# Moving the last eight heads of an output projection's weights behind the last V tile, the last ones head by head

## The chip, the cores and the metric

The kernel runs on one core of one Trainium2 chip. The metric is device time in microseconds (us), lower is better. A time is the median of several executions, every run fast, that is, not more than 1.5% above the fastest of its kernel. A profile is one execution. Its times count from the start of the span, and its span is some 2 us shorter than the measured time.

The engines are named as the profiler does: PE multiplies matrices (PEld is its loading of weights), DVE is the vector engine, ACT the scalar engine, POOL is hardly used here, and SP issues the loads, which the 16 DMA engines carry out. A load "lands" when the last of its engines has reported to the load's semaphore, a counter on which other engines wait. The "chain of waits" follows the work that ended last back from its end: at each step to what released it. PE's "granted clock" is given as a share of its full clock.

## The reference

One decode step of a transformer block for four sequences: attention over a cache of 8,192 positions, 32 heads of 128, in parallel with a gated feed-forward layer. All inputs are bf16.

```python
xn = layernorm(x)                                     # x: (4, 1, 512)
q = (xn @ wq).reshape(4, 1, 32, 128).transpose(0, 2, 1, 3)
p = softmax(einsum("bhqd,bhkd->bhqk", q, k_cache) * 128 ** -0.5)
o = einsum("bhqk,bhkd->bhqd", p, v_cache)             # caches: (4, 32, 8192, 128)
attn = o.transpose(0, 2, 1, 3).reshape(4, 1, 4096) @ wo      # wo: (4096, 512)
ffn = (silu(xn @ w_gate) * (xn @ w_up)) @ w_down
out = x + attn + ffn
```

The two caches are 537 MB, and wo is 4.2 MB. Everything has to be read once.

## The kernel before

The work is cut into 32 tiles of 4 heads of one sequence. K and V of a tile are 8.4 MB each and go through three large buffers in on-chip memory ("slots"). Every load is issued from SP's queue in program order, so the order of the calls is the order of the stream. The output of head `h` (`otn[:, h]`) is multiplied with the 128 rows of `wo` that belong to it, in four matmuls of 128 columns (`yo_mm`).

```python
def yo_mm(lhsT, rhs, start=False):
    for i in range(2):
        for a in range(2):
            c0 = a * DH + i * DQ
            mm(yo_ps[i][a * QB:a * QB + B, :], lhsT, rhs[:, c0:c0 + DQ], start=start)

def load_wo(t_):                       # heads 0..27 in 4 KB rows, heads 28..31 in 1 KB rows
    n = (NB4 - 1) * 4
    nc.sync.dma_start(out=t_[:, 0:n * D]..., in_=A_wo[0:n * P, :]...)
    nc.sync.dma_start(out=t_[:, n * D:H * D]..., in_=A_wo[n * P:H * P, :]...)
    wo_t.append(t_)
# ... tiles 0..30 in a loop; then the last one:
n = NT - 1
t_ = slot()
load_wo(t_)                            # wo
v_from(n, t_, H * D, 0, (T // 4, T // 4))   # first half of the last V, two loads
turn_k(n, (2,) * 8)
# ... scores of the last tile, PV of the tile before it
t_ = slot()
v_from(n, t_, 0, T // 2, (48, 32, 24, 16, 8))   # second half of the last V, five loads
max_1(n)
pv_still(n - 1, xps, T - 96, T)
max_2(n)
wo_some(H)                             # the 28 heads that are finished
pt_turn(n)
row_sums(n)
fin_1(JL)
pv_still(n, xps, 0, T - TL)
fin_2(JL, xps, B - 2)
pv_still(n, xps, T - TL, T)
fin_3(JL, xps)                         # normalise: otn of the last four heads
wo_ready = H
wo_some(H)                             # their product with wo
# ... copy yo_ps to res, store res in two halves (from SP and from ACT)
```

Of the kernel before, what the change touches and what calls it, by code (L numbers as in the profile page):

```python
# [15 lines left out]
def kernel(  # L16
# [13 lines left out]
    nc = tc.nc  # L30
    P = nc.NUM_PARTITIONS

    B, Sq, D = A_x.shape
    _, H, Sk, Dh = A_k_cache.shape
# [42 lines left out]
    def slot():  # L77
        return slots.tile([P, SLOT], dt.bfloat16, name="slot")
# [7 lines left out]
    def beside_wq(parts, w, dtype=dt.bfloat16):  # L86
# [13 lines left out]
                      in_=x_flat[B - 1:B, :].rearrange("b (k e) -> b k e", k=2))  # L100
# [13 lines left out]
    def v_from(n, t_, base, t0, parts):  # L114

        j, b = divmod(n, B)
        src = A_v_cache[b, j * HT:(j + 1) * HT, :, :].rearrange("h (p t) d -> (h p) (t d)", t=T)
        v_tiles[n, t0 * Dh] = (t_, base)
        for w in parts:
            nc.sync.dma_start(out=t_[:, base:base + w * Dh], in_=src[:, t0 * Dh:(t0 + w) * Dh])  # L120
            base, t0 = base + w * Dh, t0 + w
# [149 lines left out]
    NB4 = H // 4  # L271
    wo_t = []

    def load_wo(t_):
        n = (NB4 - 1) * 4
        nc.sync.dma_start(out=t_[:, 0:n * D].rearrange("p (k c e) -> p k (c e)", c=4, e=D),
                          in_=A_wo[0:n * P, :].rearrange("(k p c) e -> p k (c e)", p=P, c=4))
        nc.sync.dma_start(out=t_[:, n * D:H * D].rearrange("p (h e) -> p h e", e=D),
                          in_=A_wo[n * P:H * P, :].rearrange("(h p) e -> p h e", p=P))
        wo_t.append(t_)  # L280


    s_ps, pt, nmx, osb, rcp = {}, {}, {}, {}, {}
# [28 lines left out]
    def max_1(n):  # L312
        mx = small.tile([P, 1], dt.float32, name="mx")
        nc.vector.reduce_max(out=mx[:], in_=s_ps[n][:], axis=AX.X)  # L314
        nmx[n] = mx

    def max_2(n):

        mps = psM.tile([P, 512], dt.float32, name="mps")
        nc.tensor.matmul(mps[:, 0:P], lhsT=nmx.pop(n)[:, 0:1].to_broadcast([P, P]), rhs=ident_f[:, :],  # L320
                         is_transpose=True, start=True, stop=True, skip_group_check=True)
        nm = small.tile([P, HT], dt.float32, name="nm")
        nc.vector.tensor_reduce(out=nm[:], in_=by_row(mps[:, 0:P]), axis=AX.X, op=ALU.max, negate=True)  # L323
        nc.vector.tensor_tensor(out=nm[:], in0=nm[:], in1=rowb_q[:], op=ALU.mult)
        nb = small.tile([P, 1], dt.float32, name="nb")
        nc.vector.reduce_sum(out=nb[:], in_=nm[:], axis=AX.X)
        p_ = pp.tile([P, 512], dt.bfloat16, name="p_")
        rs = small.tile([P, 1], dt.float32, name="rs")
        nc.scalar.activation(out=p_[:], in_=s_ps.pop(n)[:], func=ACT.Exp, bias=nb[:, 0:1], scale=qscale,  # L329
                             accum_out=rs[:])  # L330
        pt[n] = p_
        rs_t[n] = (rs, mps)

    def pt_turn(n):
        p_ = pt[n]
        t_ = ptz[n % 2]
        for y in range(HT):
            nc.vector.transpose(out=t_[y * QB:(y + 1) * QB, :, y, :, :].rearrange("p s u x -> p s (u x)"),  # L338
                                in_=p_[y * QB:(y + 1) * QB, :].rearrange("p (s w) -> p s w", s=4))
        pt[n] = t_[:].rearrange("p s y u x -> p (s y u x)")  # L340
# [20 lines left out]
    def pv_still(n, xps, t0, t1, start=False):  # L361

        for t in range(t0, t1):
            k, u = divmod(t, NV)
            off = p_off(k) + u * QB
            mm(xps[:, :, n % B], v_cols(n, t * Dh, (t + 1) * Dh),
               pt[n][:, off:off + (HT - 1) * NV * QB + 1:NV * QB], start=(start and t == t0))
# [14 lines left out]
    def fin_3(j, xps):  # L382
        nc.vector.tensor_tensor(out=otn[:, j * HT:(j + 1) * HT, :], in0=xps[:], in1=rcp.pop(j)[:], op=ALU.mult)  # L383
# [12 lines left out]
    def wo_mm(i):  # L396
        yo_mm(otn[:, i, :], wo_t[0][:, i * D:(i + 1) * D])
# [7 lines left out]
    def wo_some(n):  # L405
        nonlocal wo_next
        while n > 0 and wo_next < wo_ready:
            wo_mm(wo_next)
            wo_next += 1
            n -= 1  # L410
# [47 lines left out]

    n = NT - 1
    t_ = slot()  # L460
    load_wo(t_)
    v_from(n, t_, H * D, 0, (T // 4, T // 4))
    turn_k(n, (2,) * 8)
    xps = x_tile()
# [3 lines left out]
            pv_still(n - 1, xps, (g - 7) // 2 * 32, (g - 5) // 2 * 32, start=(g == 7))  # L468
    t_ = slot()
    v_from(n, t_, 0, T // 2, (48, 32, 24, 16, 8))  # L470
    max_1(n)
    pv_still(n - 1, xps, T - 96, T)
    max_2(n)
    wo_some(H)
    pt_turn(n)
    row_sums(n)
    fin_1(JL)
# [1 line left out]
    fin_2(JL, xps, B - 2)  # L479
    pv_still(n, xps, T - TL, T)  # L480
    fin_3(JL, xps)
    wo_ready = H
    wo_some(H)
    assert wo_next == H
# [35 lines left out]
```

## Time and profile before

| | before |
|---|---|
| median of 3 runs (range) | 1285.74 us (1285.46 to 1285.93) |
| span of the profiled run | 1283.9 us |
| DMA | 551 MB at 430 GB/s |
| PE, DVE busy | 79%, 57% of the span |
| last V piece reaches PE | 1279.71 us |
| last matmul with wo ends | 1281.39 us |
| store issued by SP | 1281.70 us |

The DMA engines have no pause until the very end, so a change in the order of the loads can gain only in the last few microseconds, after the stream. The lines of the profile for this are shown and read in the prediction below.

### The profile page before, as it was taken

The page shows a single profiled execution, that of the slowest core. Times are in us where ns is not written, and L with a number is a line of the kernel's source. Part 1 is how long each engine was busy: PE and PEld are TensorE (multiplying, and loading weights), DVE is VectorE, ACT ScalarE, POOL GpSimd, SP SyncE. Part 2 cuts the span into 40 slices and gives each one's busy share as a digit, 9 for nine tenths or more (in the row PEclk, how much of TensorE's full clock was granted, in tenths as well). Part 3 has the DMA queues.
Part 4 walks back from the last instruction along what each step waited for, and adds up shares of the span by engine and source line. Part 5 has one row for each costly group of instructions (what it writes and reads, how often), then busy time and mean ns, then how long its engine had stood idle before and what let it go on. Part 6 is the DMA issues. An engine that isn't in the chain of part 4 may idle for free.

```text
span 1283.9 us, 11309 instructions
## 1 busy us (share of the span) xinstructions
PE 1008.6 (79%) x5170; PEld 462.0 (36%) x5170; DVE 736.6 (57%) x621; ACT 30.2 (2%) x71; POOL 5.9 (0%) x12
## 2 busy tenths in 40 slices
PE   1697777977778977778877779877779787789786
PEld 0254333433334433333333334333334333334345
DVE  4846644665545665554666645666445766446651
ACT  1000000000000000000000000000000000000000
POOL 1000000000000000000000000000000000000000
PEclk9897889988889988889888899888899888899886
DMA  9999999999999999999999999999999999999997
GB/s 425 423 431 430 427 443 427 436 439 427 438 427 442 427 429 443 433 425 440 439 423 431 444 428 429 443 432 425 437 435 435 431 433 440 429 425 440 437 412 318
DMA packets 12311, 551.49 MB, mean 430 GB/s; under 512 B 1244, under 2 KB 1768, under 8 KB 3048
## 3 DMA queue, kind: packets, MB, share of 16 engines
q1 hardware_dynamic: 12256, 550.78, 99.3%
q8 instruction: 40, 0.66, 0.2%
q14 instruction: 7, 0.06, 0.0%
q10 hardware_dynamic: 8, 0.00, 0.0%
HBM read 550.77 MB, written 0.00 MB: 429 GB/s over the span
## 4 chain that ended last, share of the span: by engine, by line
DMA 55%; PE 36%; DVE 9%; SPq 0%; issue 0%; ACT 0%; DVEq 0%; ACTq 0%
DMA slot<-in_A_k_cache_dram 50%; PE sps L74 19%; PE oacc L74 15%; DVE slot L301 8%; DMA slot<-in_A_v_cache_dram 5%; PE xps L74 0%; DVE ptz L338 0%; PE mps L74 0%; PE mps L320 0%; SPq L120 0%; PE yo_ps L74 0%; ACT p__5209 L329 0%; ACT p__324 L329 0%; DVE oacc L371 0%; DVE mx L314 0%
## 5 line engine op out<-in xcount | busy, mean ns | idle before, releaser
L301 DVE STREAM_TRANSPOSE slot<-slot 128x2048 uint32<-128x2048 uint32 (+1 forms) x198 | 561.8, 2901 | 286.7 <-DMA slot<-in_A_k_cache_dram 286.7
L74 PE MATMUL sps<-slot,zq 128*128 128x512 bf16 x2048 | 521.4, 418 | 237.7 <-DVE slot L301 237.6
L74 PE MATMUL oacc<-slot,ptz 128*16 128x512 bf16 x1920 | 430.8, 380 | 0.2 <-DMA slot<-in_A_v_cache_dram 0.2
L74 PEld LDWEIGHTS <-zq 128*128 128x128 bf16 x2048 | 212.3, 104 | 543.4 <-issue 232.9
L74 PEld LDWEIGHTS <-ptz 128*16 128x16 bf16 x1920 | 195.1, 106 | 209.1 <-issue 12.7
L314 DVE TENSOR_REDUCE mx<-sps 128x1 f32<-128x512 f32 x32 | 22.1, 692 | 101.7 <-PE sps L74 101.7
L74 PEld LDWEIGHTS <-slot 128*128 128x128 bf16 (+2 forms) x716 | 25.7, 110 | 27.1 <-issue 13.4
L348 DVE RECIPROCAL rcp<-mps 128x4 f32<-128x4 f32 x32 | 5.8, 182 | 44.4 <-PE mps L74 44.4
L323 DVE TENSOR_REDUCE nm<-mps 128x4 f32<-128x64 f32 x32 | 7.2, 224 | 36.0 <-PE mps L320 36.0
L74 PE MATMUL xps<-ptz,slot 128*128 128x4 bf16 x512 | 15.3, 169 | 7.5 <-DMA slot<-in_A_v_cache_dram 7.5
L74 PE MATMUL yo_ps<-slot 128*4 128x128 bf16 (+1 forms) x60 | 3.5, 309 | 14.7 <-DMA slot<-in_A_x_dram 13.1
L74 PEld LDWEIGHTS mps<-rowb,rs 128*128 128x128 f32 x64 | 9.7, 190 | 14.3 <-issue 12.4
L74 PE MATMUL mps<-rowb,rs 128*128 128x4 f32 x64 | 12.5, 266 | 1.5 <-ACT p__324 L329 1.5
L74 PE MATMUL xps<-rowy,o 128*32 128x4 f32 (+1 forms) x226 | 10.7, 205 | 2.2 <-DVE o L373 2.2
L291 DVE COPY zq<-qt 32x8 bf16<-32x8 bf16 x64 | 11.1, 174 | 0.7
L320 PE MATMUL mps<-ident_f,mx 128*128 128x128 f32 x32 | 10.4, 326 | 0.8 <-DVE mx L314 0.8
L74 PEld LDWEIGHTS xps<-rowy,o 128*32 128x32 f32 (+1 forms) x226 | 10.0, 155 | 2.8 <-DVE o L373 2.8
L320 PEld LDWEIGHTS mps<-ident_f,mx 128*128 128x128 f32 x32 | 4.3, 134 | 13.8 <-issue 6.7
L393 DVE TENSOR_TENSOR otn<-xps,rcp 32x16 bf16<-32x16 f32 x28 | 4.8, 170 | 6.6 <-PE xps L74 4.5
L383 DVE TENSOR_TENSOR otn<-xps,rcp 128x16 bf16<-128x16 f32 x1 | 0.2, 175 | 14.3 <-PE xps L74 14.3
L74 PE MATMUL yo_ps<-slot,otn 128*4 128x128 bf16 x128 | 6.1, 280 | 2.1 <-DMA slot<-in_A_wo_dram 1.8
L74 PE MATMUL mps<-xnt_w,slot 128*128 128x4 bf16 x112 | 6.8, 199 | 0.3 <-DVE rcp L348 0.3
(146 smaller groups left out, 185.9 us busy)
## 6 DMA issues: line engine op xcount, KB each, us to landing
slot<-in_A_v_cache_dram SPq DMA_DIRECT2D x2, 4096.0 KB, 32.1
slot<-in_A_wq_dram SPq DMA_DIRECT2D x1, 4096.0 KB
slot<-in_A_v_cache_dram SPq DMA_DIRECT2D x2, 2048.0 KB
slot<-in_A_wo_dram SPq DMA_DIRECT2D x1, 3584.0 KB, 31.5
slot<-in_B_w_gate_dram SPq DMA_DIRECT2D x1, 1792.0 KB, 24.5
slot<-in_B_w_up_dram SPq DMA_DIRECT2D x1, 1792.0 KB
slot<-in_B_w_down_dram SPq DMA_DIRECT2D x1, 1792.0 KB
slot<-in_A_v_cache_dram SPq DMA_DIRECT2D x1, 1536.0 KB
```

The costliest lines, as they stand in the source:

```text
L74: nc.tensor.matmul(out_ap, lhsT=lhsT, rhs=rhs, start=start, stop=True, skip_group_check=True, **kw)
L291: nc.vector.tensor_copy(out=zq[a * QB:(a + 1) * QB, :, :, XO + a * QB].rearrange("p b (j r) -> p r j b", r=2), in_=qt[a * QB:(a + 1) * QB, ...
L301: nc.vector.transpose(out=ap, in_=ap)
L314: nc.vector.reduce_max(out=mx[:], in_=s_ps[n][:], axis=AX.X)
L320: nc.tensor.matmul(mps[:, 0:P], lhsT=nmx.pop(n)[:, 0:1].to_broadcast([P, P]), rhs=ident_f[:, :], is_transpose=True, start=True, stop=True, ...
L323: nc.vector.tensor_reduce(out=nm[:], in_=by_row(mps[:, 0:P]), axis=AX.X, op=ALU.max, negate=True)
L348: nc.vector.reciprocal(out=rcp[j][:, :, b], in_=mps[:, P:P + HT])
L383: nc.vector.tensor_tensor(out=otn[:, j * HT:(j + 1) * HT, :], in0=xps[:], in1=rcp.pop(j)[:], op=ALU.mult)
L393: nc.vector.tensor_tensor(out=otn[q0:q1, j * 4:j * 4 + 4, :], in0=xps[q0:q1], in1=r_[q0:q1, y, :].unsqueeze(1).to_broadcast([QB, 4, B]), o ...
```

## The change

In the kernel before, all of wo stands in the stream in front of the last V. But the longest tail hangs on V: its last piece must be multiplied, normalised and then multiplied with wo, while a piece of wo only needs its four matmuls per head. The change puts the last eight heads of wo behind the last piece of V, the last four as 2, 1 and 1 heads, so that the last bytes of the stream are followed by as little work as possible. In return the matmuls of heads 24 to 27, which ran early, now run at the end.

```diff
-    def load_wo(t_):
-        n = (NB4 - 1) * 4
-        nc.sync.dma_start(out=t_[:, 0:n * D].rearrange("p (k c e) -> p k (c e)", c=4, e=D),
-                          in_=A_wo[0:n * P, :].rearrange("(k p c) e -> p k (c e)", p=P, c=4))
-        nc.sync.dma_start(out=t_[:, n * D:H * D].rearrange("p (h e) -> p h e", e=D),
-                          in_=A_wo[n * P:H * P, :].rearrange("(h p) e -> p h e", p=P))
-        wo_t.append(t_)
+    def load_wo(k0, k1):
+        nc.sync.dma_start(out=wo_t[0][:, k0 * 4 * D:k1 * 4 * D].rearrange("p (k c e) -> p k (c e)", c=4, e=D),
+                          in_=A_wo[k0 * 4 * P:k1 * 4 * P, :].rearrange("(k p c) e -> p k (c e)", p=P, c=4))
+
+    def load_wo_heads(h0, h1):
+        nc.sync.dma_start(out=wo_t[0][:, h0 * D:h1 * D].rearrange("p (h e) -> p h e", e=D),
+                          in_=A_wo[h0 * P:h1 * P, :].rearrange("(h p) e -> p h e", p=P))
 ...
     t_ = slot()
-    load_wo(t_)
+    wo_t.append(t_)
+    load_wo(0, NB4 - 2)
     v_from(n, t_, H * D, 0, (T // 4, T // 4))
 ...
     v_from(n, t_, 0, T // 2, (48, 32, 24, 16, 8))
+    load_wo(NB4 - 2, NB4 - 1)
+    load_wo_heads(H - 4, H - 2)
+    load_wo_heads(H - 2, H - 1)
+    load_wo_heads(H - 1, H)
     max_1(n)
     pv_still(n - 1, xps, T - 96, T)
     max_2(n)
-    wo_some(H)
+    wo_some(H - 8)
 ...
     fin_3(JL, xps)
+    wo_some(H)
     wo_ready = H
     wo_some(H)
```

## The prediction

> **What bounds the kernel now.** I read four views in this order: the page's slices, the chain of waits in the last 35 us, the instructions of the last 4 us in order of time, and the stretches of the end with their DMA share. The slices come first because they say which resource is full:
>
> ```profile
> DMA  9999999999999999999999999999999999999997
> GB/s 425 423 431 430 427 443 427 436 439 427 438 427 442 427 429 443 433 425 440 439 423 431 444 428 429 443 432 425 437 435 435 431 433 440 429 425 440 437 412 318
> ```
>
> The DMA engines are full in 39 of 40 slices at about 430 GB/s; only the last slice has a hole. The kernel reads 551 MB once and cannot read less, so 1,280 of its 1,284 us are the stream. The diff does not change the bytes. What is left to gain is what happens after the last byte, and the chain of waits shows that (start us, us, what):
>
> ```profile
> 1253.34 0.33 SPq L120
> ...
> 1255.92 23.15 DMA slot<-in_A_v_cache_dram
> 1279.07 0.05 issue
> 1279.11 0.59 PE xps L74 x16
> 1279.71 0.01 issue
> 1279.71 0.39 PE xps L74 x8
> 1280.11 0.02 issue
> 1280.13 0.19 DVE otn L383
> 1280.32 0.04 issue
> 1280.36 1.03 PE yo_ps L74 x16
> 1281.39 0.02 issue
> 1281.42 0.26 ACT res L489
> ```
>
> The last pieces of V release the last PV products (x16 and x8), these the normalisation (otn), this the product with the last four heads of wo (16 matmuls), and this the copy and the store. I take the landing of the last V piece as 1279.71 us: the x16 group takes 0.59 us for 16 matmuls and the x8 group 0.39 for 8, and the packet records of the trace show the last V packet 0.64 us after the last packet of the piece before it, which released the PE at 1279.07. So 1281.39 - 1279.71 = 1.68 us of work depend on the last byte, up to the end of wo; from there to the end of the span at 1283.9 there are 2.5 us of copy and store that the diff does not touch.
>
> **The queue ahead of that byte.** On SP's queue the end of the stream is V of tile 30, wo (4 MB), the first half of V of tile 31 (4 MB) and its second half in five pieces (4 MB). The packet records give the time of one packet by size: 4 KB 0.159 us, 1 KB 0.046 us, 16 KB 0.61 us. They also show that the 16 engines do not finish together: seven finish V some 7 us before the other nine. The stretches show the same (busy PE, PEld, DVE, ACT, POOL; then granted clock, DMA share, GB/s):
>
> ```profile
> 1260.00:1270.00 10.00, 6.10 (x163) 5.80 (x158) 2.95 (x5) 0.00 (x0) 0.00 (x0) 0.84 1.00 423
> 1270.00:1275.00 5.00, 3.19 (x113) 3.10 (x113) 0.00 (x0) 0.00 (x0) 0.00 (x0) 0.50 0.75 310
> 1275.00:1280.00 5.00, 3.17 (x84) 2.82 (x82) 0.00 (x0) 0.00 (x0) 0.00 (x0) 0.50 0.43 176
> ```
>
> The share falls to 0.43 while the chain still waits for V. A load spread over all engines lands with the slowest one, so the slow engines are what counts, each with 1/16 of every load.
>
> **What the Trainium skill says.** "DMA: Bandwidth & Descriptors", section "Queues, rings and completion order", says that on each DMA engine the descriptors of one ring are consumed in ring order. The trace agrees: wo lands at 1258.8, the quarters of V at 1265.05 and 1269.91, the 48-column piece at 1273.59, as issued. So moving a load back moves up everything it stood before, by its own packet time. The same page's "Rules for kernel authors" says that transfers under 64 KB are mostly overhead and asks for 1 MiB or more; the head loads here are 128 KB. In the trace a load that queues behind others costs its packets and little else: the 256 KB V piece comes 0.64 us after its forerunner, and 8 packets of 2 KB at 0.084 us are 0.67. "Trainium Kernel Development and Optimization", section "Key Constraints", says that all queues run on the same 16 engines; a load on ACT's queue would gain no bandwidth either. "TensorE: Matmul & The Clock Gate", part 1, says that PE runs at half clock until it has been busy for some 3.4 us. The trace shows 0.50 granted in the two last stretches, so I take the tail's own matmul times, not those of the middle.
>
> **The change part by part.**
>
> (1) Two loads of wo (28 heads in 4 KB rows, 4 heads in 1 KB rows) become five: 24 heads in front of V as before; behind the last V piece 4 heads in 4 KB rows, then 2, 1 and 1 heads in 1 KB rows. Packets per engine are the same: before 56 of 4 KB and 32 of 1 KB, after 48 + 8 of 4 KB and 32 of 1 KB. Added are three completion writes of about 0.01 us. The last landing of the whole stream stays at 1279.71 + 0.03 = about 1279.75.
>
> (2) What moves behind V is 8 x 0.159 + 32 x 0.046 = 1.27 + 1.47 = 2.74 us per engine. The last V piece lands at 1279.71 - 2.74 = 1276.97, and all earlier pieces of V equally earlier (the first quarter at 1262.3, the 48-column piece at 1270.85).
>
> (3) PE's early wo work shrinks from 112 matmuls (5.08 us from 1258.80) to 96: 5.08 x 96/112 = 4.35 us, beginning with the landing at 1258.8 - 1.27 = 1257.5 and ending at about 1261.9. The transposed probabilities are ready at 1258.53 + 2.85 = 1261.4, and row sums take 0.4. PE is then ready for V's first quarter exactly as it lands, and the DMA stays the bound.
>
> (4) The new end. V at 1276.97, PV 0.39, normalisation 0.02 + 0.19 + 0.04: otn is ready at about 1277.65. Heads 24 to 27 land at 1276.97 + 1.27 = 1278.25, heads 28 and 29 at + 16 x 0.046 = 1279.0, head 30 at 1279.35, head 31 at 1279.75. The tail issues one small matmul per 0.05 us (16 weight loads in 0.73 us) and the last one takes 0.31 to come out. Heads 24 to 27 then run from 1278.25 to about 1279.0, heads 28 and 29 to 1279.4, head 30 to 1279.6; PE is free when head 31 lands. Four matmuls cost 1.03 - 12 x 0.05 = 0.43, so wo ends at 1279.75 + 0.05 + 0.43 = 1280.23 instead of 1281.39.
>
> Sum: 1.68 us after the last byte become about 0.52, minus 1.16 us. Nothing else on the path changes: the order of instructions on DVE and ACT is identical, and PE only has 16 matmuls moved.
>
> (5) A wait in the program that could undo it. The compiled program rotates eight completion semaphores over the loads, so a load is not issued before the eighth load ahead of it has landed. In the kernel before this shows in the queue's own waits:
>
> ```profile
> SPq L120 <- DMA slot<-in_A_wo_dram: 2.4, 1, 2.4
> ```
>
> The last V piece waited for wo there. After the change the four trailing loads wait for the first wo load, the first and second quarter of V, and the 48-column piece: about 1257.5, 1262.3, 1267.2 and 1270.85. Head 31 is thus issued 1270.85 + 0.4, some 8 us before its turn on a slow engine (1279.4). The fast engines are done with V some 7 us earlier, at about 1270, and may idle for it, which costs nothing since the slow ones set the landing.
>
> **The rivals.** (a) Late issue: if the last loads reached the engines late, each would stand alone and pay a start; the queue's small loads show about 2 us from issue to landing (the store: from 1281.70 to 1283.9), so the end would move by +1 to +2 us, to about 1286 to 1287. Against it stand the 8 us of slack just worked out, and that the stream has been queued 20.9 us deep at the end (issue to landing of the last V piece). (b) PE becomes the bound: eight heads are 32 matmuls after the normalisation, 1277.65 + 32 x 0.05 + 0.31 = 1279.6 if all weights were there, before head 31 has landed. Only if the slow clock made one matmul 0.064 us apart (1.03/16) would heads 24 to 31 run 1278.25 + 2.05 = 1280.3 plus latency, and the gain be 0.8 to 1.1. (c) The tail's landing is ruled by a slow engine that differs from run to run, and the 1.2 us drown: the three runs span 1285.46 to 1285.93, so a shift of 1.2 is two and a half times their spread, visible but below 0.1% of the time. (d) The small 1 KB rows become slower at the end, with nine engines left: they are in both kernels, and a packet's time is set by its own engine, since 16 KB takes about 0.61 us early and late. This would cost below 0.3 us.
>
> **Range and chances.** 1285.74 - 1.16 = 1284.6 us. With the spread of runs of 0.5 us, rival (b) at -0.8 and rival (a) at +1 on one side, and a clean landing of -1.7 plus a lucky run on the other, I take 1283.4 to 1286.0. Two per cent would be 25.7 us; nothing here can move that, only a stall of the whole stream. Faster 0.005, same 0.985, slower 0.01.
>
> **What would show it right or wrong.** Right: the wait for the last V piece in the chain ends 2.5 to 3 us earlier; the chain's last DMA is wo, not V; four matmuls onto yo_ps follow it within about 0.5 us; the last stretch's DMA share is unchanged. Wrong: the trailing loads issued after 1275 us (rival a), or PE without a pause from heads 24 on (rival b), or V landing where it did (the load order would not matter on a slow engine), or a last landing more than 0.3 us later (the small loads have a cost that I set to nothing).

## The result

The changed kernel took 1285.01 us (median of 4 runs, 1284.70 to 1285.09), the kernel before 1285.70 us (4 runs, 1285.46 to 1285.93). That is 0.69 us less, inside the predicted range of 1283.4 to 1286.0. But that range holds the times of the kernel before, too, so lying inside it says little; the traces must test the mechanism. Ratios are the mean time of one kernel's fast runs over that of the other's of the same rounds, so not quite the ratio of the medians quoted: here 0.9995, 95% interval 0.998 to 1.0009. The interval is far wider than the spread of the runs. I rely on the spread: over all rounds the 14 runs of the changed kernel lie between 1284.61 and 1285.09 us, and no run of the kernel before is under 1285.41.

The chain of waits of the changed kernel, to be read against that of before (start us, us, what):

```profile
1257.44 20.81 DMA slot<-in_A_wo_dram
1278.24 0.04 issue
1278.29 1.90 PE yo_ps L74 x32
1280.18 0.02 issue
1280.21 0.26 ACT res L497
```

V, the PV products and the normalisation are gone from the chain. It now goes from the landing of a piece of wo straight to 32 matmuls with wo, and these end at 1280.18 instead of 1281.39. The stretches of the end (busy PE, PEld, DVE, ACT, POOL; granted clock, DMA share, GB/s):

```profile
1270.00:1275.00 5.00, 2.89 (x82) 2.71 (x82) 0.00 (x0) 0.00 (x0) 0.00 (x0) 0.50 0.77 304
1275.00:1280.00 5.00, 3.48 (x80) 3.15 (x80) 0.17 (x1) 0.00 (x0) 0.00 (x0) 0.50 0.44 162
```

The DMA share is nearly the same as before (0.75 and 0.43). The stream ends when it did: by the semaphore records of the two traces its last load lands at 1279.67 us in both. Only its order differs.

So 1.21 us were gained at the last matmul, but the measured time shows 0.69 (0.82 and 0.98 in two later rounds). Part of the difference is visible in the end of the program. The waits of SP's queue show the last wait for the stores, first before, then after (queue and line, waited for, us in total, times, longest):

```profile
SPq L515 <- DMA out_dram<-res: 0.7, 1, 0.7
```

```profile
SPq L523 <- DMA out_dram<-res: 1.1, 1, 1.1
```

A longer wait is not yet a later end. SP's own records in the traces, in nanoseconds after the store's issue, show what happens:

```
                before                               after
wait for 104, 103    340                             1203, until 1396
wait for 107, 102    405                             1433
wait for 108, 101    466, until 1198                 1495
wait for 109, 100   1235                             1559
wait for 110, 106   1372                             1620
end sequence        1437                             1685
last instruction    2185                             2433
store (SP) lands    1176 on semaphore 101            1186 on semaphore 104
store (ACT) lands   1355 on semaphore 110            1374 on semaphore 103
```

At its end SP looks at the semaphores of all loads (and at two others, 100 and 106) in a fixed order, two at a time, about 0.06 us for each pair that needs no wait. The stores land equally late in both. Before, the semaphores of the two stores stood in the third and the last pair, so nearly all others had been looked at while the stores were under way. After, they are in the first pair, and the other four pairs follow one by one once the stores have landed: 2.43 - 2.19 = 0.25 us lost. Which semaphore a store gets follows from the rotation of eight over all loads; the change adds three loads, and so moves the stores' place by three.

The rest comes from which execution was profiled: the profiled run of the changed kernel took 1284.70 us, the fastest of its four and 0.31 us under their median. For the 13 profiled runs other than that of before, the time of the profiled execution is the end of wo plus the time from the store's issue to the end plus 2.07 to 2.18 us. So profiles and times agree run by run, and a difference of 0.1 to 0.3 us between a profile and a median is the choice of the run.

### The profile page after: what moved, and what is told of

Its sections match the earlier page's. It is cut to its first block, busy times and chain, and to the rows that moved or that the text cites. A ratio compares the mean times of both kernels' runs of the same rounds, so it can differ in the third digit from the quotient of the medians.

```text
span 1282.9 us, 11312 instructions
## 1 busy us (share of the span) xinstructions
PE 1012.6 (79%) x5170; PEld 464.0 (36%) x5170; DVE 736.6 (57%) x621; ACT 30.1 (2%) x71; POOL 5.9 (0%) x12
## 4 chain that ended last, share of the span: by engine, by line
DMA 54%; PE 37%; DVE 8%; issue 0%; ACT 0%; SPq 0%; DVEq 0%
DMA slot<-in_A_k_cache_dram 50%; PE sps L74 19%; PE oacc L74 17%; DVE slot L303 8%; DMA slot<-in_A_wo_dram 4%; PE mps L74 0%; PE mps L322 0%; DVE ptz L340 0%; PE yo_ps L74 0%; ACT p__324 L331 0%; DVE mx L316 0%; SPq L96 0%; SPq L98 0%; ACT res L497 0%; SPq L99 0%
## 5 line engine op out<-in xcount | busy, mean ns | idle before, releaser
L74 PEld LDWEIGHTS <-otn 128*4 128x4 bf16 x128 | 6.7, 123 | 1.6 <-issue 1.5
```

The costliest lines, as they stand in the source:

```text
L74: nc.tensor.matmul(out_ap, lhsT=lhsT, rhs=rhs, start=start, stop=True, skip_group_check=True, **kw)
```

## The experiments

Kernels are compared only within the same rounds. Columns: median, difference to the median of before in the same rounds, end of the last matmul with wo in the profiled run, time from the store's issue to the last instruction, and the semaphores of the stores (SP, ACT).

| run | median us | to before | wo ends | issue to end | semaphores |
|---|---|---|---|---|---|
| before | 1285.70 | | 1281.39 | 2.19 | 101, 110 |
| after | 1285.01 | -0.69 | 1280.18 | 2.43 | 104, 103 |
| e0_after | 1284.71 | -0.82 | 1280.25 | 2.43 | 104, 103 |
| e1_four_heads_one_load | 1285.19 | -0.34 | 1280.79 | 2.29 | 102, 101 |
| e2_four_behind | 1284.37 | -1.16 | 1280.04 | 2.36 | 103, 102 |
| e4_pe_moved_only | 1286.35 | +0.82 | 1281.84 | 2.42 | 104, 103 |
| e3_split_only | 1285.94 | +0.33 | 1281.40 | 2.43 | 104, 103 |
| e5_quarter_heads | 1288.76 | +3.15 | 1284.54 | 2.18 | 101, 110 |
| p1_eight_rows_alone | 1298.21 | +12.60 | 1294.05 | 2.43 | 104, 103 |
| p2_more_instructions | 1287.31 | +1.70 | 1282.90 | 2.36 | 103, 102 |
| e6_four_behind_fewer_loads | 1284.25 | -1.44 | 1280.09 | 2.18 | 101, 110 |
| e7_after_fewer_loads | 1284.29 | -1.40 | 1280.06 | 2.19 | 101, 110 |
| e8_four_behind_again | 1284.44 | -1.25 | 1280.19 | 2.36 | 103, 102 |
| e9_after_again | 1284.71 | -0.98 | 1280.10 | 2.43 | 104, 103 |

All results were correct. The four calls had before at 1285.70, 1285.53, 1285.61 and 1285.69 us.

### How large the gain is

`e0_after` and `e9_after_again` are the changed kernel itself.

> The changed kernel again, beside the kernel before on the same chip, to fix the size of the gain. Theory (1.68 us of work after the last byte become about 0.5): 0.7 to 1.2 us faster than the kernel before, wo ends near 1280.2 us of the span instead of 1281.4. Rival c (noise): no shift beyond 0.3 us.

> The changed kernel once more, as a reference on the same chip: 0.7 to 0.9 us faster than the kernel before.

Measured 0.82 and 0.98 us faster, the second a little more than expected. The profile's parts add up: the end of wo moved by -1.14 (e0) and -1.29 (e9), the end sequence by +0.24 and +0.25, together -0.90 and -1.04.

### The head by head part

```diff
-    load_wo_heads(H - 4, H - 2)
-    load_wo_heads(H - 2, H - 1)
-    load_wo_heads(H - 1, H)
+    load_wo_heads(H - 4, H)
```

> Undoes only the head by head part: the last four heads come in one load of 512 KB, still behind V. Theory (the last landing sets the end): all 16 matmuls of these heads wait for the landing at about 1279.7 and take 1.03 us, so wo ends at about 1280.75, 0.55 us later than in the changed kernel and 0.6 us before the kernel before. Rival b (PE bound: its 32 matmuls ran without a pause from 1278.29): PE would be no later, wo ends at 1280.2 as in the changed kernel.

Measured 1285.19 us, 0.48 us slower than the changed kernel on the same chip. The chain of waits (start us, us, what):

```profile
1279.71 0.04 issue
1279.75 1.03 PE yo_ps L74 x16
1280.79 0.02 issue
1280.81 0.26 ACT res L495
```

The sixteen matmuls wait for the one landing at 1279.71 and then take their 1.03 us, to the hundredth as expected, and wo ends 0.54 us later than in e0. The changed kernel's last load lands at 1279.67, and by then most of these 16 matmuls have run: in its trace the four of head 31, the last, start at 1279.74.

### Only four heads behind V

```diff
-    load_wo(0, NB4 - 2)
+    load_wo(0, NB4 - 1)
 ...
-    load_wo(NB4 - 2, NB4 - 1)
     load_wo_heads(H - 4, H - 2)
 ...
-    wo_some(H - 8)
+    wo_some(H - 4)
```

> Only the last four heads behind V (2, 1, 1), heads 24 to 27 stay in front. V lands 1.27 us later than in the changed kernel, otn at about 1278.9, 16 matmuls to about 1280.0, head 31 lands at 1279.7. Theory (last landing sets the end): wo ends at 1280.1 to 1280.2, the same time as the changed kernel within 0.2 us. Rival b (PE bound by its 32 matmuls): half the matmuls after otn, so 0.3 us or more faster than the changed kernel. A third view, that each KB moved behind V is worth its transfer time: 1.2 us slower than the changed kernel.

> The version with four heads behind V once more, as a reference on the same chip: 1.0 to 1.2 us faster than the kernel before, 0.3 us faster than the changed kernel.

Measured 0.34 us (e2) and 0.27 us (e8) faster than the changed kernel, in separated ranges in e2 (1284.35 to 1284.54 against 1284.62 to 1284.88). The theory (within 0.2 us) missed, rival b (0.3 us or more) fits better, and the third view is out. Against before, e8 gained 1.25 us, a little more than expected. The chain of e2:

```profile
1278.34 0.39 PE xps L74 x8
1278.72 0.02 issue
1278.75 0.18 DVE otn L385
1278.93 0.04 issue
1278.98 1.06 PE yo_ps L74 x16
```

V lands 1.25 us later than in the changed kernel, but only 16 matmuls follow the normalisation. No landing of wo stands in this chain, since the chain follows a group of matmuls from its first one. A wait inside the group shows only in the records of the trace: in e2 the last load lands at 1279.60, and the matmuls of head 31 start at 1279.64, after a pause of 0.07 us (in e8 1279.75, 1279.80 and 0.11 us). From the last landing to the end of wo 0.44 us pass in e2 and in e8, but 0.51, 0.65 and 0.64 us in the three profiled runs of the changed kernel, where PE is still busy with other heads when head 31 lands. So with four heads behind V the last landing sets the end; with eight it is PE, with its 32 matmuls after the landing of heads 24 to 27 at 1278.24, and rival b was right by 0.07 to 0.21 us. With the 0.07 us of the end sequence (2.36 against 2.43) this makes 0.14 to 0.28 of the 0.27 to 0.34 us measured. The profiled ends of wo alone do not rank the two (1280.04 against 1280.25 in the first pair, 1280.19 against 1280.10 in the second), because the last landing itself differs from execution to execution, from 1279.46 to 1279.75 in these runs.

### The two halves of the change alone

`e3_split_only` has the five loads, all in front of V, and the old order on PE. `e4_pe_moved_only` is the same, but with the new order on PE.

```diff
     load_wo(0, NB4 - 2)
+    load_wo(NB4 - 2, NB4 - 1)
+    load_wo_heads(H - 4, H - 2)
+    load_wo_heads(H - 2, H - 1)
+    load_wo_heads(H - 1, H)
     v_from(n, t_, H * D, 0, (T // 4, T // 4))
 ...
-    wo_some(H - 8)          # e3 only; e4 keeps this line
+    wo_some(H)
```

> wo in the changed kernel's five loads, but all of them in front of V, and the matmuls in the old order (28 heads early). Theory (the number of loads costs nothing, only their place counts): the kernel before within 0.2 us, wo ends at about 1281.4. Rival: if five loads cost some fixed time each on the DMA engines, 0.3 us or more slower than before.

e3 was 0.33 us slower than before (1285.71 to 1286.14 against 1285.41 to 1285.88, so the ranges overlap); the theory "loads cost nothing" missed and its rival seemed right. The end of its chain, and the wait for the stores:

```profile
1280.37 1.04 PE yo_ps L74 x9
1281.40 0.02 issue
```

```profile
SPq L523 <- DMA out_dram<-res: 1.1, 1, 1.1
```

So wo ends at 1281.40, within 0.01 us of before: the DMA engines lost nothing. The loss lies after the store, 2.43 us instead of 2.19, with the changed kernel's semaphores.

> The wrong half of the change alone: all of wo is loaded in front of V as before (in the five pieces), but the matmuls of the last eight heads run after otn. Theory: otn stays at about 1280.3, 32 matmuls take 1.90 instead of 1.03 us, so wo ends at 1282.2 and the kernel is about 0.9 us slower than before. If PE's order did not matter: as before.

e4 was 0.82 us slower than before, and its chain is:

```profile
1279.65 0.38 PE xps L74 x8
1280.03 1.82 PE yo_ps L74 x32
1281.84 0.02 issue
1281.87 0.26 ACT res L497
```

The total looks as expected, but for another reason. The 32 matmuls begin at 1279.95 (the chain counts them from the end of the group before, 1280.03), while the normalisation only starts at 1280.06: heads 24 to 27 belong to an earlier group and do not need it, so PE fills that gap with them. The end of wo moves by only 0.45 us (0.87 expected), and the other 0.24 are the end sequence. Together that is 0.69 by the profile, 0.82 by the times.

### Late issue

The prediction's first rival. The last four heads come in 16 loads of 32 partitions, so that the rotation of eight semaphores makes each of the last eight wait for a load that is still near.

```diff
-    load_wo_heads(H - 4, H - 2)
-    load_wo_heads(H - 2, H - 1)
-    load_wo_heads(H - 1, H)
+    for h in range(H - 4, H):
+        for q in range(4):
+            nc.sync.dma_start(out=wo_t[0][q * QB:(q + 1) * QB, h * D:(h + 1) * D],
+                              in_=A_wo[h * P + q * QB:h * P + (q + 1) * QB, :])
```

> The changed kernel with the last four heads cut into 16 loads of 32 KB (32 partitions each), so that the rotation of eight semaphores makes the last eight of them wait for loads that land less than 3 us earlier. Theory (rival a of the prediction, late issue, has an edge here): the eighth waits for heads 24 to 27 at about 1278.2 and lands at about 1280.3, the last one at about 1282; wo ends at 1282 to 1283, 1.7 to 2.7 us slower than the changed kernel and 0.9 to 1.9 slower than before. If late issue cannot hurt because the queue is always full: as the changed kernel within 0.3 us.

Measured 3.15 us slower than before, more than expected. The end of the chain of waits:

```profile
1281.58 0.04 issue
1281.63 0.42 SPq L477
1282.05 0.04 issue
1282.09 1.92 DMA slot<-in_A_wo_dram
1284.01 0.14 issue
1284.14 0.40 PE yo_ps L74 x4
```

The edge is real. The part I had left out is SP itself: once the eighth of the 16 loads could go, at 1278.47, SP issued the eight after it at 0.46 us each (0.42 and a gap of 0.04), and the last one, alone on idle engines, needed 1.92 us to land. The changed kernel stays clear of this: its last load is issued by 1271.2 (8.89 us of issues and waits from 1262.31).

### Why half of the DMA engines are late

The packet and semaphore records point to the cause of the 7 us between the early and the late engines. Over the whole run the landings of one load spread over the 16 engines more and more: by 0.4 us at first, by 1.3 to 1.8 us up to some 280 us, then by about 3, 4.4, 5.8 and at last 7.2 us, while seven engines stay together within 0.7 us. So the late engines (eight at 7 us, one at 4) fall back in steps of about 1.4 us, and the instruction queue has 40 packets of 16 KB spread over the run, five for each of eight engines: their durations, 0.88 to 0.97 us, repeat with every eighth packet. The spread grows at the packets of 41.3, 292.2, 583.4, 874.6 and 1161.0 us, the first of each round of eight, and with each packet between these about one more engine is among the last. From the page of the kernel before (queue, kind: packets, MB, share):

```profile
q8 instruction: 40, 0.66, 0.2%
```

The Trainium skill, "Runtime: NRT & Kernel Launch", section "Instruction fetch mechanics", says that an engine's instruction memory is refilled in blocks of 16 KiB, 256 instructions, by DMA. The page of the profile counts 10,340 instructions of PE and PEld here, which is 40.4 blocks: the 40 packets agree. To test it I added 1,856 small matmuls and their weight loads to the version with four heads behind, where PE has time to spare:

```diff
         nc.vector.reciprocal(out=rcp[j][:, :, b], in_=mps[:, P:P + HT])
+        if 2 <= n < NT - 1:
+            for _ in range(64):
+                mm(mps[0:16, 256:260], pt[n][:, 0:16], xnt_w[:, 0, 0:4], start=True)
```

> Why nine DMA engines are late. In the packet records of the kernel before, 40 instruction fetches of 16 KB lie on the DMA engines, and the late engines fall back in steps of some 1.3 us at their times. This version (four heads behind V) has 1856 small matmuls with their weight loads more, put where PE has idle time, 3712 instructions. Theory: about 14 or 15 fetches more on eight engines, each of them 1.8 times 1.3 = 2.3 us later; the early engines as they were; the kernel 2 to 2.5 us slower than the version with four heads behind. Rival (the engines' delay is their own and has nothing to do with instructions): no change beyond 0.3 us. PE's added busy time is about 0.1 us x 1856 = some 100 to 180 us, below its idle time of some 270.

It has 15 fetches more, 40 + 3,712/256 = 54.5 rounded up:

```profile
q8 instruction: 55, 0.90, 0.2%
```

By the semaphore records the seven early engines finish the last V piece 9.7 us ahead of the last engine instead of 6.8 in e2. They are as early as there (the last of the seven at 1271.45 against 1271.49), so the stream as such was not held up by PE's added work; the late ones alone are later. The kernel is 1.70 us slower than before, that is 2.86 us slower than e2 (each against before). Fifteen fetches on eight engines are two for most, and 2 x 1.4 = 2.8, a little above the 2 to 2.5 expected. PE's added busy time was only 49 us. So the kernel's end is set by the DMA engines that also fetch instructions.

Could the loads be shared out unequally, to help the late engines? A probe: the second half of the last V as 120 partitions, and the last eight partitions in one load of their own.

```diff
-    v_from(n, t_, 0, T // 2, (48, 32, 24, 16, 8))
+    v_from(n, t_, 0, T // 2, (T // 2,), P - 8, P)
+    v_from(n, t_, 0, T // 2, (48, 32, 24, 16, 8), 0, P - 8)
```

> Probe on the version with four heads behind V: which DMA engines are the late ones. The second half of the last V comes as partitions 0 to 119 in five loads and partitions 120 to 127 in one load of eight 32 KB rows. If that load runs on eight engines that belong to the seven early ones mostly, its packets lie some 7 us ahead of the late engines' packets of the same place in the queue, and the end stays or comes earlier; if on the late ones, its packets are all late and the kernel is about 1.2 us slower than the version without the probe.

It was 12.6 us slower than before, far off both guesses. Of the eight single rows five started early and three late, so a load of few partitions does not pick out the early engines. And the packets of the loads of 120 partitions slowed, by 1.4 to 1.8 times: a 12 KB packet took 0.83 us (median) instead of 0.46. The 1 KB packets of wo behind them hardly did (0.049 instead of 0.046). By the semaphore records these loads ran on 15 engines and the load of eight rows on eight; why the packets slow is not settled by this run.

### A version that beats both

If the end sequence costs what the semaphores' place says, giving the stores their old semaphores is worth 0.25 us in the changed kernel and 0.18 in the version with four heads behind. Merging loads moves the rotation back, by three in the one and two in the other:

```diff
-    v_from(n, t_, H * D, 0, (T // 4, T // 4))
+    v_from(n, t_, H * D, 0, (T // 2,))
 ...
-    v_from(n, t_, 0, T // 2, (48, 32, 24, 16, 8))
+    v_from(n, t_, 0, T // 2, (64, 40, 16, 8))
```

```diff
-    nc.sync.dma_start(out=x_sb[0:B - 1, :], in_=x_flat[0:B - 1, :])
-    nc.sync.dma_start(out=x_sb[B - 1:B, :].rearrange("b (k e) -> b k e", k=2),
-                      in_=x_flat[B - 1:B, :].rearrange("b (k e) -> b k e", k=2))
+    nc.sync.dma_start(out=x_sb[0:B, :], in_=x_flat[0:B, :])    # e7 only
```

`e7_after_fewer_loads` is the changed kernel with both edits; `e6_four_behind_fewer_loads` is e2 with the first alone.

> The changed kernel with three loads fewer (x in one load, the first half of the last V in one, its second half as 64, 40, 16, 8), which gives the stores the kernel before's semaphores again. Theory: wo ends at 1280.2 as in the changed kernel, from the store's issue to the end 2.18 instead of 2.43 us, so 0.2 to 0.35 us faster than the changed kernel. Rival: no difference to the changed kernel.

> Candidate: four heads behind V, and two loads fewer (the first half of the last V in one load, its second half as 64, 40, 16, 8), so that the two stores get the semaphores that SP's end sequence looks at last, as in the kernel before. Theory (the end after the stores depends on which semaphores they got: 2.18 us from the store's issue to the end with those of the kernel before, 2.36 in the version with four heads behind): 0.15 to 0.3 us faster than the version with four heads behind, 1.3 to 1.5 us faster than the kernel before; issue to end 2.18 us. Rival (these 0.2 us are the store's own noise): as the version with four heads behind.

e7 took 1284.29 us (1284.26 to 1284.37), 0.42 us less than the changed kernel beside it (1284.61 to 1284.95), and issue to end fell from 2.43 to 2.19 us as expected, the time by a little more than the 0.2 to 0.35 us expected. The wait of SP's queue is back at its old value:

```profile
SPq L521 <- DMA out_dram<-res: 0.7, 1, 0.7
```

The end of wo moved by another 0.04 us, so 0.29 us are accounted for, as much as lies between the two profiled executions (1284.62 and 1284.33); the remaining 0.13 of the medians is the choice of these executions, 0.09 us under the one median and 0.04 over the other. e6 took 1284.25 us, 0.19 us less than e8 beside it; its issue to end is 2.18 instead of 2.36. e6 and e7 differ by 0.04 us, less than their spread. Both beat the kernel before, by 1.44 and 1.40 us, and the changed kernel by 0.46 and 0.42. That is 0.1% of the time.

## Why the prediction was right or wrong

- **What bounds the kernel: right.** The stream ends at the same time (DMA shares 0.77 and 0.44 in the last stretches, 0.75 and 0.43 before), and only the work behind it changed.
- **Step 1, the same packets and an unmoved last landing: right.** It is at 1279.67 before and after; 1279.75 was predicted.
- **Step 2, V earlier by its neighbours' packet time: right.** The last V piece reached PE at 1277.06 (its group of 24 matmuls starts at 1276.47, and the first 16 take 0.59 as before; 1276.97 was predicted), the second quarter at 1267.25 instead of 1269.91, a shift of 2.66 (2.74 predicted).
- **Step 3, early wo work of 4.35 us: mis-sized.** The 96 matmuls took 5.28 us, since PE's granted clock over them was 0.51, while the 5.08 us for 112 that the step scaled down were run at 0.63; and PE reached the first quarter of V at 1262.92, about 0.6 us after its predicted landing. It cost nothing, since PE then waited 2.51 us for the next quarter.
- **Step 4, the new end: the time right, partly by luck.** wo ended at 1280.18 (1280.23 predicted), but not for the reason given. PE was not free when head 31 landed at 1279.67: heads 24 to 27 began at 1278.29, heads 28 and 29 at 1279.15 (a wait of 0.05 us for their load), head 30 at 1279.53 and head 31 at 1279.74, where the step had PE waiting from 1279.6. In e0 there was no pause at all, the sign named for rival b. So rival b was right in kind and small in size: PE ended 0.07 us later than the last landing would have allowed, 0.2 us in e0 and e9. An earlier landing (1279.67 for 1279.75) hid it in the sum. Rival b in turn put all 32 matmuls behind the normalisation; e4 shows that heads 24 to 27 do not wait for it.
- **The failed term: "2.5 us of copy and store that the diff does not touch".** The diff does touch it. Three more loads turn the rotation of semaphores, and the end sequence after the stores grew by 0.25 us. That leaves -1.21 + 0.25 = -0.96 us by the profile, against the -1.16 of the sum; the times show -0.69, -0.82 and -0.98.
- **A reading for rival a: wrong.** The 2 us from a store's issue to its landing (1281.70 to 1283.9) reach to the end of the span; the store landed 1.18 us after its issue. A lone load of 32 KB did take 1.92 us in e5, so the size of the rival stands.
- **Step 5, the semaphore wait has slack: right.** e5 takes the slack away and loses 4 us against the changed kernel's place (+3.15 against -0.82). SP's issue time of 0.46 us per load was missing in the reasoning.
- **Rival c, the gain drowns: wrong.** The runs separate, though no 2% rule sees it. **Rival d, slow small rows: did not show**, as the 1 KB packets took 0.046 us in both places.

## What to carry to other kernels

When the DMA stream is the bound, order its last bytes by the length of the work behind them: what has the longest chain goes first, what needs four matmuls goes last, in pieces, until PE is as late as the stream. Count the loads, too: with semaphores in rotation a few loads more decide both whether the last issues are late and where the stores stand in the end sequence. And a step that "the diff does not touch" is worth one look after the change, since a fifth of the gain at the last matmul was lost there. As more instructions on PE brought the end back (p2), fewer should bring it forward; no run here tried that.

## What the Trainium skill lacked or had wrong

- "Runtime: NRT & Kernel Launch", section "Instruction fetch mechanics", calls the fetch of instructions mostly hidden. For PE's own progress no run contradicts this, but in a kernel bound by DMA it is not free: each 16 KB block puts its DMA engine back by about 1.4 us, 40 blocks on eight engines make these 7 us late at the end, and 15 more blocks cost 2.86 us.
- "Trainium Kernel Development and Optimization", section "Key Constraints", says that issuing from several queues only saves the sequencer's issue time, and gives no size for it. Here it was large: eight small loads issued in a row kept SP for 0.46 us each, 3.7 us in all (e5).
- No page was found that says in what order SP waits at the end of a program: here it waits for the loads' semaphores two at a time in a fixed order, some 0.06 us a pair, so from the store's issue to the end 2.18, 2.29, 2.36 or 2.43 us pass, by the semaphores that the stores got.
- "DMA: Bandwidth & Descriptors", section "Rules for kernel authors", calls transfers under 64 KB mostly overhead. The overhead depends on the queue: the first six 32 KB loads of e5, still behind other packets, landed 0.15 to 0.17 us apart, of which their two packets on each engine are 0.09; the last one, issued late on idle engines, took 1.92 us.
